# A decoder block of two layers: w_down in two long runs per partition, gate and up columns in a step of seven, and new orders

## The chip, the cores and the metric

The kernel runs on one core of a Trainium2 chip. Its five engines run side by side: TensorE (PE) for matmuls, VectorE (DVE), ScalarE (ACT), GpSimd (POOL), and SyncE (SP), which here only issues DMAs. Each has its own queue of instructions and works through it in order; semaphores tie the queues together. Sixteen DMA engines move data from the main memory into the on-chip memory SBUF (128 partitions). Matmul results land in PSUM. The metric is the device time of one execution in microseconds (us). "Slower" or "faster" is said of a difference over 2%.

## The reference

Four tokens, one per sequence, go through attention, FFN, attention, FFN. Both attentions use the same caches and weights, and so do both FFNs.

```
attention(x): q = x @ wq                      # 16 heads of 256
              k, v = the last 2048 rows of the caches, 8 heads, each used by two heads of q
              o = softmax(q k^T / 16) v
              return o @ wo                   # 4096 -> 448
ffn(x):       return (silu(x @ w_gate) * (x @ w_up)) @ w_down    # 448 -> 1792 -> 448

x = A_x                                       # 4 x 448, bf16
x = x + attention(layernorm(x));  x = x + ffn(layernorm(x))
x = x + attention(layernorm(x));  x = x + ffn(layernorm(x))
```

The window of K and V is 67 MB, more than SBUF holds. Most of it is read for the first attention; what is still in SBUF when the second one comes is used again, and the rest is read a second time.

## The kernel before, in words

The program is a graph of 1465 operations, each with an engine, its inputs and its outputs. The order on each engine is not worked out in the program: it is written out in the lists `SEQ_PE`, `SEQ_DVE`, `SEQ_ACT`, `SEQ_POOL` and `SEQ_SP`, made beforehand by a planner. `schedule` (L240) reads them, puts every K and V load into a slot of SBUF by the list `SLOTS`, makes each load wait for the last reader of what stood in its slot, and places the semaphore waits.

- **Attention.** A pair of heads is a group (`group`, from L957). Each head's K comes in two loads of half a megabyte (L976), each of which DVE transposes in place (L982); V comes in two loads too (L992). PE makes scores (L1016), DVE and PE find the maximum (L1031 to L1045), ACT takes the exponential (L1049), PE turns it (L1060) and multiplies with V (L1090). `out_proj` (L1135, L1143) multiplies with wo and adds into the PSUM bank A.
- **Slots.** There are 31 slots of half a megabyte, and seven more in the space of wq, which come free only after the last query projection of the last token (L683). In each token's first attention, six of eight heads keep their K and V for the second one.
- **FFN of one token** (`ffn`, L783), as soon as its first attention is done. The norm (L589 to L629) feeds the gate and up matmuls (L801). They compute the 1792 hidden values as 14 chunks of 128: for each chunk and each of four pieces of the 448 inputs, 128 columns of w_gate or w_up are loaded into the array as weights, and a small moving operand (32 columns) passes. Gate and up take 112 such pairs together. ACT makes the tanh (L832), DVE the product (L835, L846), and `down_part` (L853) multiplies with w_down, chunk by chunk. Then come the next norm and the query projection (L683 to L722), without which no group of the token's second attention can start.
- The FFNs of tokens 0 to 3 after the first attention are separate; the last FFN takes all four tokens at once and ends the kernel. A second form of the FFN, `ffn_row` (L726), exists in the code, but neither `ROWF` nor `PLAN` names a token for it, so it emits nothing.
- **w_down's layout.** The chunk number of a hidden value is its number divided by 128, its place in the chunk the remainder. SBUF partition p therefore holds rows p, 128 + p, 256 + p and so on, each of 448 values, 896 bytes in a row:

```
            load(rank_d, 1605632, wd_sb[:, :, :], B_w_down.rearrange("(c p) n -> p c n", p=128), "wd", 430)
```

- **Fillers.** A "w" in `SEQ_PE` is a matmul with zero weights into bank A (L1253), put where the planner expected PE to be idle. `HELD` ties operations that read bank A to the fillers.

Of the kernel before, what the change touches and what calls it, by code (L numbers as in the profile page):

```python
# [6 lines left out]
ALU = mybir.AluOpType  # L7
# [6 lines left out]
B = 4  # L14
# [36 lines left out]
ROWF = ()  # L51
# [35 lines left out]
).split()  # L87
SEQ_DVE = (
# [18 lines left out]
).split()  # L107
SEQ_ACT = (
# [5 lines left out]
).split()  # L114
SEQ_POOL = (
# [8 lines left out]
).split()  # L124
SEQ_SP = (
# [243 lines left out]
def build(nc, A_x, A_k_cache, A_v_cache, A_wq, A_wo, B_x, B_w_gate, B_w_up, B_w_down, out):  # L369
# [3 lines left out]
    with ExitStack() as es:  # L373
# [788 lines left out]
        for si, heads in enumerate(rest):  # L1162
# [57 lines left out]
            for t, layer in full:  # L1220
# [7 lines left out]
                if layer == 0:  # L1228
                    if rowf:
# [4 lines left out]
                        for u in with_:  # L1234
                            final(u, pos)
# [94 lines left out]
```

## Time and profile before

| | |
|---|---|
| median of three runs | 278.97 us (278.21 to 281.98) |
| the profiled execution | 279.5 us |
| its span, first to last instruction | 277.7 us |
| mean granted TensorE clock | 0.969 |
| data moved | 96.68 MB, mean 348 GB/s |

The profile is of one execution, so durations are set against 279.5 us, not against the median. In its tables an engine's name with q (SPq) is the engine's sequencer issuing a DMA; PEld is the loading of weights into the array, which runs beside PE's matmuls. A line number stands for the line of the code that made the instruction, and tiles are named "out<-in". In a table by stretch the columns are: the stretch, its length, then for PE, PEld, DVE, ACT and POOL the busy time with the number of instructions, then the granted clock, the busy share of the DMA engines, and GB/s. In a timeline the columns are start, duration, engine, line, operation, tiles, shapes and count; neighbours of one kind are merged into one row, and in brackets stands how long the engine was idle ahead of it and what ended that. The duration of a merged row runs to the end of its last instruction.

### The profile page before, as it was taken

To read this page: it belongs to the slowest core of one execution; us is meant where nothing else is said; L and a number is where in the kernel's file an instruction comes from. 1 tells how busy PE (TensorE), PEld (TensorE's weight loads), DVE (VectorE), ACT (ScalarE), POOL (GpSimd) and SP (SyncE) were. 2 spreads that over 40 slices of the span, in tenths; PEclk is the share of its full clock that TensorE was granted. 3 is DMA by queue.
4 is the path that set the end of the run, shared out by engine and by line. 5 is a ranking of instruction groups with operands and counts; after the bars stand their busy time and mean duration, and the time that the engine had idled before them with its cause. 6 is when DMAs were issued, how large, how long until landed. Compare 5 with 4: busy or idle time off the path is not lost.

```text
span 277.7 us, 9966 instructions
## 1 busy us (share of the span) xinstructions
PE 209.0 (75%) x4424; PEld 125.0 (45%) x4424; DVE 173.8 (63%) x522; ACT 47.3 (17%) x115; POOL 76.5 (28%) x195
## 2 busy tenths in 40 slices
PE   0000076699788968988998897899699798899997
PEld 0000032355464634455754444474454356456694
DVE  7973056445545799368447995655789845559751
ACT  0000000232111220121113221211022031032510
POOL 1000017142204412421253342124132332043650
PEclk9999999999989999999999999999979999599998
DMA  7999999999999999999799999939999999589200
GB/s 292 394 419 412 403 412 406 402 396 401 389 379 405 357 396 415 407 409 353 260 332 410 409 405 411 405 150 362 362 417 407 410 408 346 215 279 408 79 5 1
DMA packets 28474, 96.68 MB, mean 348 GB/s; under 512 B 2828, under 2 KB 6928, under 8 KB 27792
## 3 DMA queue, kind: packets, MB, share of 16 engines
q1 hardware_dynamic: 28423, 96.06, 88.8%
q8 instruction: 34, 0.56, 0.8%
q14 instruction: 9, 0.07, 0.1%
q10 hardware_dynamic: 8, 0.00, 0.0%
HBM read 96.05 MB, written 0.00 MB: 346 GB/s over the span
## 4 chain that ended last, share of the span: by engine, by line
PE 43%; DMA 25%; DVE 13%; SPq 10%; issue 4%; ACT 3%; POOL 2%; ACTq 0%
DMA half<-in_A_k_cache_dram 16%; PE A L1253 10%; DMA half<-in_A_v_cache_dram 9%; PE S L1016 8%; DVE half L982 7%; PE Y L1090 6%; SPq L992 5%; PE Z L801 4%; SPq L976 3%; PE Z L683 3%; SPq L558 2%; PE Z L853 2%; PE A L1143 2%; PE Y L1060 2%; PE A L1135 2%
## 5 line engine op out<-in xcount | busy, mean ns | idle before, releaser
L982 DVE STREAM_TRANSPOSE half<-half 128x1024 uint32<-128x1024 uint32 x80 | 97.2, 1231 | 22.3 <-DMA half<-in_A_k_cache_dram 22.2
L1253 PE MATMUL A<-identb,small 128*128 128x512 bf16 x223 | 67.4, 404 | 0.3 <-DVE xr L903 0.3
L1103 POOL TENSOR_TENSOR small<-small 128x4 f32<-128x4 f32 x32 | 32.5, 1017 | 70.1 <-DVE small L1081 64.7
L1090 PE MATMUL Y<-half,pT 128*8 128x256 bf16 x1024 | 38.7, 275 | 3.2 <-issue 1.4
L1016 PE MATMUL S<-half,qe 128*8 128x256 bf16 (+1 forms) x1120 | 35.3, 269 | 6.3 <-issue 2.0
L1016 PEld LDWEIGHTS S<-half,qe 128*8 128x8 bf16 x1120 | 24.4, 84 | 16.2 <-issue 3.8
L1023 POOL TENSOR_TENSOR qe<-qc,small 128x64 bf16<-128x64 bf16 x56 | 15.3, 295 | 47.6 <-PE S L1016 33.9
L921 PE MATMUL Z<-identb,wo_sb 4*128 4x4 bf16 x4 | 0.3, 167 | 36.7 <-DMA wo_sb<-in_A_x_dram 36.7
L1031 DVE TENSOR_REDUCE small<-S 104x1 bf16<-104x256 f32 x32 | 13.4, 417 | 22.0 <-PE S L1016 22.0
L1090 PEld LDWEIGHTS Y<-half,pT 128*8 128x8 bf16 x1024 | 21.3, 85 | 12.0 <-DVE small L1081 3.2
L1253 PEld LDWEIGHTS A<-identb,small 128*128 128x128 bf16 x223 | 19.1, 103 | 14.9 <-issue 6.4
L1105 ACT ACTIVATE oh<-Y 128x256 bf16<-128x256 f32 x32 | 12.2, 383 | 36.2 <-PE Y L1090 27.2
L615 POOL TENSOR_SCALAR st<-st 128x1 f32<-128x1 f32 x16 | 4.5, 280 | 50.1 <-DVE st L609 50.1
L1107 DVE SCALAR_TENSOR_TENSOR oh<-oh,small,Y 128x256 bf16<-128x256 bf16 x32 | 15.0, 469 | 4.0 <-ACT oh L1105 3.8
L921 PEld LDWEIGHTS Z<-identb,wo_sb 4*128 4x128 bf16 x4 | 0.2, 104 | 36.6 <-DMA wo_sb<-in_A_x_dram 36.6
L1143 PE MATMUL A<-wo_sb,oT 128*4 128x448 bf16 x200 | 13.8, 352 | 1.3 <-DVE oT L1123 1.3
L1049 ACT ACTIVATE praw<-S,small 104x256 bf16<-104x256 f32 x16 | 7.6, 472 | 38.9 <-DVE small L1045 38.9
L1049 ACT ACTIVATE praw<-S,small,st 104x256 bf16<-104x256 f32 x16 | 9.0, 564 | 30.1 <-DVE small L1045 26.6
L1068 ACT ACTIVATE pT<-Y 128x192 bf16<-128x192 f32 x32 | 10.5, 329 | 15.5 <-PE Y L1060 14.1
L683 PE MATMUL Z<-half,small 128*5 128x512 bf16 x160 | 10.9, 379 | 1.5 <-DVE small L592 1.4
L1081 DVE TENSOR_REDUCE small<-Y 128x4 f32<-128x64 f32 x32 | 6.7, 213 | 7.8 <-PE Y L1076 7.6
L1060 PE MATMUL Y<-selt,praw 104*64 104x48 bf16 x256 | 10.1, 197 | 1.8 <-ACT praw L1049 1.7
(135 smaller groups left out, 245.8 us busy)
## 6 DMA issues: line engine op xcount, KB each, us to landing
half<-in_A_v_cache_dram SPq DMA_DIRECT2D x80, 512.0 KB, 13.5
half<-in_A_k_cache_dram SPq DMA_DIRECT2D x76, 512.0 KB, 10.7
wo_sb<-in_A_wo_dram SPq DMA_DIRECT2D x8, 448.0 KB, 11.8
half<-in_A_wq_dram SPq DMA_DIRECT2D x3, 1024.0 KB, 16.2
half<-in_A_k_cache_dram SPq DMA_DIRECT2D x2, 1024.0 KB, 6.4
wd_sb<-in_B_w_down_dram SPq DMA_DIRECT2D x1, 1568.0 KB, 18.5
wu_sb<-in_B_w_up_dram SPq DMA_DIRECT2D x1, 1344.0 KB, 11.8
wg_sb<-in_B_w_gate_dram SPq DMA_DIRECT2D x1, 1344.0 KB, 14.7
```

What stands on the lines that cost most here:

```text
L683: last = e.matmul(zb[32 * j:32 * j + B + 1, 0:512], lhsT=lhsT, rhs=wq_sb[:, c:c + 512], start=(cc == 0), stop=(cc == 3), skip_group_check= ...
L982: return e.transpose(a, a)
L992: g.dma(pp + VLAG, 1 << 19, lambda e, cell=cell, hv=hv, vsrc=vsrc: e.dma_start(unit(cell), vsrc[hv]), None, w=(f"v{t}_{kvh}_{hv}",), run=4 ...
L1016: last = e.matmul(Sb[s_][qd:qd + 8, c0:c0 + rhs.free_size()], lhsT=qe[q_][:, P, ce, :, :].rearrange("p a n -> p (a n)"), rhs=rhs, start=(c ...
L1023: g.op(*((DVE, 0.13) if layer and fresh.get(t, gi) == gi else (POOL, 0.25)), pos - SLEAD - 1, lambda e, P=P, t=t, kvh=kvh: e.tensor_tensor ...
L1049: return e.activation(praw[0:R, 0:128 * n].rearrange("p (g r l) -> p g r l", g=2 * n, l=2), Sb[s_][0:R, 0:128 * n].rearrange("p (l g r) -> ...
L1060: last = e.matmul(Yb[p_][64 * h:64 * h + 64, c0:c0 + (48 if n == 2 else 32)], lhsT=praw[0:R, 64 * gg:64 * gg + 64], rhs=w, start=(gg == 0) ...
L1090: last = e.matmul(Yb[p_][32 * gg:32 * gg + M, 256:512], lhsT=pT[pt][:, gg, 2 * a + hv, 4 * P:4 * P + M] if n == 2 else p1[:, gg % 2, 2 * a ...
L1103: g.op(POOL, 0.69, pos, lambda e: e.tensor_tensor(ri[p_][:, 0:2 * n], rs[p_][:, 0:2 * n], expo[:, 1:1 + 2 * n], op=ALU.pow), r=(f"rs{p_}", ...
L1107: g.op(DVE, 0.43, pos, lambda e: e.scalar_tensor_tensor(out=oh[:, :], in0=oh[:, :], scalar=lomask[:, 0:1], in1=Yb[p_][:, 256:512], op0=ALU ...
L1143: last = e.matmul(Ab[32 * k:32 * k + B, 0:D], lhsT=oT[oi][:, k % 2, k // 2, :], rhs=wo_sb[:, 4 * kvh + k, :], start=False, stop=False, ski ...
L1253: return e.matmul(Ab[:, 0:512], lhsT=zero[:, 0:1].broadcast_to([128, 128]), rhs=identb[:, :].unsqueeze(1).broadcast_to([128, 4, 128]), sta ...
```

## The change

Four things change.

- **The load of w_down.** Hidden value number 896 h + 7 p + j now goes to partition p, chunk 7 h + j. A partition's seven rows of one half then stand side by side in the main memory, and it gets two runs of 6272 bytes instead of 14 of 896.
- **Gate and up.** Chunk 7 h + j now holds the columns 896 h + j + 7 p, so the 128 columns that are loaded as weights are taken in a step of seven instead of one. The numbers of matmuls and weight loads stay, and everything between (tanh, product, the sums of columns kept for the norm) works on chunks as before.
- **`ffn_row`** and what called it are removed.
- **The orders.** All five lists, `SLOTS` and `HELD` are new. The operations are the same; PE has 233 fillers instead of 223, and the last six loads, rather than five, go into the space of wq.

```
-            load(rank_d, 1605632, wd_sb[:, :, :], B_w_down.rearrange("(c p) n -> p c n", p=128), "wd", 430)
+            load(rank_d, 1605632, wd_sb[:, :, :].rearrange("p (h j) n -> p h (j n)", h=2),
+                 B_w_down.rearrange("(h p j) n -> p h (j n)", h=2, j=7), "wd", 6272)
...
                         if cc < 3:
-                            lhsT, x = w[:, cc * FF + fc * 128:cc * FF + fc * 128 + 128], xn[:, cc, sl]
+                            c, x = cc * FF + fc // 7 * 896 + fc % 7, xn[:, cc, sl]
                         else:
-                            lhsT = w[:, 3 * FF + (fc % 7) * 128:3 * FF + (fc % 7) * 128 + 128]
-                            x = xe[:, fc // 7, sl]
+                            c, x = 3 * FF + fc % 7, xe[:, fc // 7, sl]
+                        lhsT = w[:, c:c + 890:7]
                         last = e.matmul((Zb, Z2)[gi][:, k * m * fc:k * m * fc + k * m], lhsT=lhsT,
```

Of the orders, PE's around the FFNs of tokens 1 and 3, by operation number. For token 1, 559 to 568 are gate and up, 655 the scores of a group, 572 to 575 the down projection, 590 to 598 the query; for token 3 they are 1163 to 1172, 1276, 1176 to 1179 and 1194 to 1202.

```
token 1
- 559 560 561 548 627 628 552 562 w w w w w 564 565 566 567 655 563 568 657 w 572 573 574 660 575
+ 559 548 560 561 w 627 628 552 562 564 563 565 566 567 568 w 655 572 573 574 575
token 3
- 1152 1163 1164 1156 1231 1165 1168 1169 1166 1167 1232 1233 1170 1171 1172 w w w w w w 1276 1176 1177 1278 1178 1179
+ 1163 1164 1165 1152 w w w w w 1156 1231 1166 1232 1167 1168 1169 1233 1170 1171 1172 w w w w w w 1176 1177 1178 1179 1276
```

More of the change, by code (lines that the diff above doesn't have):

```diff
@@ L50 @@
 DSTART = 2.1
-ROWF = ()
 COLX = {(3, 1): 2}
@@ L135 @@
     "0 1 2 3 4 5 6 7 8 9 10 11 12 13 14 15 16 17 18 19 20 21 22 23 24 25 26 27 28 29 30 3 4 19 21 22 14 20 9 7 10 21 "
[3 rows of a table removed]
[3 rows of a table added]
 ).split()
 HELD = (
-    "0 44 44 44 94 94 99 99 115 115 119 122 139 139 145 145 195 195 201 201 208 208 213 213 215 215 215 215 215 215 "
-    "215 215"
+    "0 45 45 46 88 89 98 98 116 116 121 126 146 146 152 152 201 201 206 206 220 220 224 224 227 227 227 227 227 227 "
+    "227 227"
 ).split()
@@ L724, in qproj @@
                     ("z2",), tuple(f"qc{t}_{h}" for h in range(HKV)), 0.18, ("Z2",))
-        def ffn_row(ts, rank):
-            rowvec(rvec[:, 1:2], "rvf", ts, rank)
-            g.op(POOL, 0.27, rank, lambda e: e.tensor_single_scalar(rvec[:, 2:3], rvec[:, 1:2], 0.5, op=ALU.mult),
-                 r=("rvf",), w=("rvs",))
-            g.op(POOL, 0.27, rank, lambda e: e.tensor_scalar(rvec[:, 3:4], rvec[:, 1:2], rvec[:, 2:3], None, op0=ALU.mult),
-                 r=("rvf", "rvs"), w=("rvt",))
-            def gu(e, gi, c0, c1):
-                last = None
-                w, zb = (wg_sb, wu_sb)[gi], (Zb, Z2)[gi]
-                for cc in range(c0, c1):
-                    for j in range(4):
-                        f0, f1 = 512 * j, min(512 * j + 512, FF)
-                        if cc < 3:
-                            parts = [(xn[:, cc, 0:B], cc * FF + f0, 0, f1 - f0)]
-                        else:
-                            parts = []
-                            for h in range(2):
-                                a, b = max(f0, 896 * h), min(f1, 896 * h + 896)
-                                if a < b:
-                                    parts.append((xe[:, h, 0:B], 3 * FF + a - 896 * h, a - f0, b - a))
-                        for lhsT, c, o, m in parts:
-                            last = e.matmul(zb[32 * j:32 * j + B, o:o + m], lhsT=lhsT, rhs=w[:, c:c + m],
-                                            start=(cc == 0), stop=(cc == 3), skip_group_check=True)
-                return last
-            for gi, (z, bank, w) in enumerate((("z", "Z", "wg"), ("z2", "Z2", "wu"))):
-                g.op(PE, 1.28, rank, lambda e, gi=gi: gu(e, gi, 0, 3), r=XN[0:B] + (w + "a",), w=(z,), bank=(bank,))
-                g.op(PE, 0.5, rank, lambda e, gi=gi: gu(e, gi, 3, 4), r=XE[0:B] + (w + "b",), acc=(z,), bank=(bank,))
-            g.op(SCA, 0.65, rank, lambda e: e.activation(wide[:, :], Zb[:, :], ACT.Tanh, scale=rvec[:, 2:3]),
-                 r=("z", "rvs"), w=WIDE, bank=("Z",))
-            vec(rank, lambda e: e.scalar_tensor_tensor(out=wide[:, :], in0=wide[:, :], scalar=1.0, in1=Zb[:, :],
-                                                       op0=ALU.add, op1=ALU.mult), ("z",), WIDE, 0.65, ("Z",))
-            vec(rank, lambda e: e.scalar_tensor_tensor(out=wideb[:, 0:512], in0=wide[:, :], scalar=rvec[:, 3:4], in1=Z2[:, :],
-                                                       op0=ALU.mult, op1=ALU.mult), ("z2", "rvt"), WIDE, 0.65, ("Z2",))
-            def turn(e):
-                last = None
-                for c in range(4):
-                    last = e.matmul(Zb[:, 16 * c:16 * c + 16].rearrange("p (j t) -> p j t", j=4),
-                                    lhsT=wideb[:, 128 * c:128 * c + 128], rhs=idt, start=(c == 0), stop=True,
-                                    skip_group_check=True)
-                return last
-            g.op(PE, 0.12, rank, turn, r=WIDE + ("identb",), w=("z",), bank=("Z",))
-            vec(rank, lambda e: e.tensor_copy(hT[:, :], Zb[:, 0:64]), ("z",), ("wb",), 0.13, ("Z",))
-            def down(e):
-                last = None
-                for c in range(4):
-                    for j in range(4):
-                        if 4 * j + c < NFC:
-                            last = e.matmul(Ab[32 * j:32 * j + B, 0:D], lhsT=hT[:, 16 * c + 4 * j:16 * c + 4 * j + 4],
-                                            rhs=wd_sb[:, 4 * j + c, :], start=False, stop=False, skip_group_check=True)
-                return last
-            g.op(PE, 1.5, rank, down, r=("wb", "wd"), acc=tuple(f"row{t}" for t in ts), bank=("A",))
@@ L1163, in build @@
             where = {}
-            if not heads:
-                g.tag = ("f", waiting[-1])
-                ffn_row(waiting, pos)
-                for u in waiting:
-                    rows(u, pos)
-                    residual(u, pos)
-                    final(u, pos)
-                g.tag = None
-                waiting = []
-                continue
             for batch in heads:
@@ L1222, in build @@
                 pos = pos_ - CROSS
-                with_ = []
-                rowf = t in ROWF and layer == 0
                 late = (t, layer) in LATE or layer == 1 and t in fin
                 residual(t, pos, late)
-                norm(t, pos, xr, None if rowf or (layer and not late) else fin.index(t) if layer else -1, late)
+                norm(t, pos, xr, None if layer and not late else fin.index(t) if layer else -1, late)
                 if layer == 0:
-                    if rowf:
-                        ffn_row(with_ + [t], pos)
-                        for u in with_ + [t]:
-                            rows(u, pos)
-                            residual(u, pos, u == t and t in QLATE)
-                        for u in with_:
-                            final(u, pos)
-                    else:
-                        ffn(with_ + [t], pos, late, False)
+                    ffn([t], pos, late, False)
                     norm(t, pos, xr, late=t in QLATE)
```

126 rows, old and new, of tables (SEQ_ACT, SEQ_DVE, SEQ_PE, SEQ_POOL) are left out of this document.

## The prediction

> **What bounds the kernel now.** I read the page first, its totals and its forty slices, to see which resource is full and where it is not.
>
> ```profile
> span 277.7 us, 9966 instructions
> PE 209.0 (75%) x4424; PEld 125.0 (45%) x4424; DVE 173.8 (63%) x522; ACT 47.3 (17%) x115; POOL 76.5 (28%) x195
> PEclk9999999999989999999999999999979999599998
> DMA  7999999999999999999799999939999999589200
> DMA packets 28474, 96.68 MB, mean 348 GB/s; under 512 B 2828, under 2 KB 6928, under 8 KB 27792
> q1 hardware_dynamic: 28423, 96.06, 88.8%
> ```
>
> The DMA engines are full in most slices, with three holes and an empty end. So the time is a stream of 96 MB, plus the time in which the stream starves, plus a tail of computing. The table of busy time by stretch puts numbers on it (GB/s stands last in a row).
>
> ```profile
> 67.00:74.00 7.00, 5.46 (x129) 3.10 (x121) 3.34 (x14) 1.98 (x6) 1.23 (x3) 1.00 1.03 407
> 74.00:81.00 7.00, 6.16 (x155) 4.62 (x155) 4.16 (x14) 0.27 (x1) 1.42 (x4) 0.76 1.07 361
> 81.00:88.00 7.00, 5.96 (x129) 3.73 (x128) 3.23 (x14) 1.40 (x3) 2.35 (x5) 1.00 1.03 407
> 90.00:97.00 7.00, 6.27 (x172) 4.37 (x176) 5.36 (x14) 1.73 (x5) 3.05 (x11) 1.00 0.94 355
> 125.00:147.00 22.00, 20.02 (x494) 13.19 (x486) 12.94 (x44) 3.37 (x9) 7.05 (x20) 1.00 0.89 319
> 180.00:194.00 14.00, 13.18 (x323) 8.94 (x319) 7.96 (x34) 2.06 (x5) 4.35 (x12) 1.00 0.67 261
> 234.00:250.00 16.00, 14.62 (x308) 8.55 (x307) 9.20 (x29) 2.69 (x6) 4.40 (x12) 0.79 0.70 241
> 250.00:259.00 9.00, 8.44 (x207) 5.69 (x211) 8.64 (x27) 2.83 (x7) 4.06 (x13) 1.00 0.92 370
> ```
>
> Undisturbed, the stream runs at 407. Against that, 90 to 97 lacks (407-355)/407 x 7 = 0.9 us, 125 to 147 lacks 4.8, 180 to 194 lacks 5.0 and 234 to 250 lacks 6.5: 17.2 us in all. Each hole lies at the FFN of one token, because slots come free only through attention that waits for the next query. After 259 nothing is left to load, and 19 us of computing follow. The chain that ended last says whose work this is:
>
> ```profile
> PE 43%; DMA 25%; DVE 13%; SPq 10%; issue 4%; ACT 3%; POOL 2%; ACTq 0%
> DMA half<-in_A_k_cache_dram 16%; PE A L1253 10%; DMA half<-in_A_v_cache_dram 9%; PE S L1016 8%; DVE half L982 7%; PE Y L1090 6%; SPq L992 5%; PE Z L801 4%; SPq L976 3%; PE Z L683 3%; SPq L558 2%; PE Z L853 2%; PE A L1143 2%; PE Y L1060 2%; PE A L1135 2%
> ```
>
> L801, the gate and up matmuls, holds 4% of the chain, 11 us. That is where the change touches the computing.
>
> **The load of w_down.** It goes from 1792 rows of 896 bytes to 256 of 6272; the bytes are the same.
>
> ```profile
> L558 SPq DMA_DIRECT2D wd_sb<-in_B_w_down_dram x1: 1398/1398/1398, 63.2 to 63.2; - x1
> DMA to landing us min/median/max: 18.5/18.5/18.5
> ```
>
> ```profile
> 58.58 0.43 SPq L558 DMA_DIRECT2D wo_sb<-in_A_wo_dram  x1
> 63.16 1.40 SPq L558 DMA_DIRECT2D wd_sb<-in_B_w_down_dram  x1
> 64.60 10.86 SPq L976 DMA_DIRECT2D half<-in_A_k_cache_dram  x1
> ```
>
> It is issued at 63.2 and lands at 81.7, so its packets end the slow stretch of 74 to 81. If 6272-byte rows move like the neighbours on both sides, the stretch shrinks by (407-361)/407 x 7 = 0.8 us; if they move no faster, by 0. The packets of 4 KB that fill the neighbours are the nearest row, so I take 0.8. SP's issue should fall from 1.40 to about 0.43, the price of a wo_sb load of 256 rows, but the next instruction on SP then sits 10.86 us, waiting for a slot: worth nothing.
>
> [...]
>
> Who uses the 0.8? PE is in order, so its timeline at token 0 tells:
>
> ```profile
> 77.52 0.91 PE L801 MATMUL Z<-small,wg_sb 128*128 128x32 bf16 x28
> 80.99 0.20 PE L1039 MATMUL S<-identb,small 104*104 104x32 bf16 x1
> 81.71 1.22 PE L853 MATMUL Z<-wide,wd_sb 128*128 128x32 bf16 x42 [0.52 <-DMA wd_sb<-in_B_w_down_dram]
> ```
>
> Token 0's down projection stands 0.52 us for w_down. That wait goes, so token 0's query and the slots it frees (the hole at 90) move up by 0.5, while the stream reaches the hole 0.8 earlier. From 97 on the stream is full to 125, so what it gained passes on. I book -0.7, between 0.5 and 0.8; bounds 0 and -0.8.
>
> **Gate and up columns in a step of seven.** No instruction is added: 112 weight loads and 112 matmuls per FFN, five FFNs. Only the address step of the weight load changes, from 2 to 14 bytes. No load with that step is in the trace, so I bound it. By shape, and on the weight-load timeline:
>
> ```profile
> L801 PEld LDWEIGHTS Z<-small,wg_sb 128*128 128x128 bf16 x280 | 8.3, 99 | 1.0 <-DVE small L875 0.8 <-issue 0.2
> L703 PEld LDWEIGHTS Z<-small,wide 128*128 128x128 bf16 x32 | 1.3, 97 | 2.4 <-ACT wide L694 1.1 <-DVE wide L691 1.0 <-issue 0.2
> L602 PEld LDWEIGHTS Z<-st,small 128*128 128x128 f32 x32 | 5.1, 196 | 3.6 <-DVE st L599 1.7 <-DVE small L592 1.0 <-DVE small L1081 0.4
> ```
>
> ```profile
> 268.16 0.78 PEld L801 LDWEIGHTS Z<-small,wg_sb 128*128 128x128 bf16 x28
> 191.74 0.17 PEld L703 LDWEIGHTS Z<-small,wide 128*128 128x128 bf16 x4 [0.22 <-issue]
> 245.58 0.30 PEld L602 LDWEIGHTS Z<-st,small 128*128 128x128 f32 x2
> ```
>
> From start to start, a contiguous load takes (0.78-0.099)/27 = 25 ns; L703, which takes every second column, (0.17-0.097)/3 = 24 ns: a step of two costs nothing. The dearest full-size load is L602's, in fp32: 0.30-0.196 = 104 ns. So a strided load lies between 25 ns (below that only if a wider step could be quicker than a contiguous one, for which I have no reason) and 104. L703 is the only strided weight load here, so I take 25, cost 0. The upper end is dear, since almost all of it is on the chain: tokens 1, 2, 3 and the last FFN hold 4 x 112 = 448 loads, at 25 ns the 11.2 us that the chain shows. At token 0, gate and up end at 78.43, over 2 us before w_down is there: a cover that hides one slow FFN. At 104 ns the rest pays 448 x 79 ns = 35 us.
>
> **The orders.** SP's first 45 entries are the same and w_down stays 54th; later loads swap places, and slots with them. PE has 233 fillers (L1253) instead of 223. Two changes fall into holes of the stream, and are priced from PE's timeline:
>
> ```profile
> 131.39 1.24 PE L1253 MATMUL A<-identb,small 128*128 128x512 bf16 x5
> 132.46 1.55 PE L801 MATMUL Z<-small,wu_sb 128*128 128x32 bf16 x56
> ```
>
> ```profile
> 238.66 2.72 PE L1253 MATMUL A<-identb,small 128*128 128x512 bf16 x6
> 241.31 1.51 PE L1016 MATMUL S<-half,qe 128*8 128x256 bf16 x32
> 242.76 0.87 PE L853 MATMUL Z<-wide,wd_sb 128*128 128x32 bf16 x28
> ```
>
> With them go SP's issue of the loads that those scores free, the last transpose of the chain, and the stretch's granted clock (ahead of DMA share and GB/s):
>
> ```profile
> 243.25 1.39 SPq L976 DMA_DIRECT2D half<-in_A_k_cache_dram  x3
> ```
>
> ```profile
> 256.98 1.15 DVE half L982
> ```
>
> ```profile
> 235.40:242.30 6.90, 6.13 (x96) 3.02 (x96) 4.01 (x6) 0.27 (x1) 0.70 (x2) 0.51 0.68 235
> ```
>
> Token 1: the five fillers between gate and up go (132.46-131.39 = 1.1 us), one comes ahead; its chain gains 0 to 0.9. I take -0.5, since the activation behind it must still be awaited. Token 3: five fillers are added ahead (1.1), and the scores of the group behind go from ahead of the down projection to behind it. Down and query come 1.5 - 1.1 = 0.4 earlier; but those scores free slots, so four loads come 1.1 + 1.4 = 2.5 later (1.4 is the 56 down matmuls), and on SP all others queue behind them. Six loads rather than five go into the space of wq, free only after the last query; the last K tile is the eighth of the final ten rather than the seventh, one load of 0.52 MB at 407 GB/s, 1.3 us. So it lands up to 3.8 us later. What hides this is DVE, busy 8.64 of 9 us from 250 to 259; in the chain the last transpose starts at 256.98, 2.7 us after the seventh load can land (243.25 + 2 + 7 x 1.3 = 254.3, with 2 us to landing as my estimate). Loss 0 to 1.1; I take +0.3.
>
> On the clock I take 0: it fell to 0.51 under token 3, so that six fillers took 2.72 us instead of 6 x 0.215 = 1.3. Five full-width fillers ahead may hold it up (-2) or only cost (already counted). The other swaps, those of DVE, ACT and POOL among them, I put at 0, within -3 and +3, a sixth of the starved 17.2 either way: no row prices them. The removed row form issued nothing.
>
> Sum: -0.7 + 0 - 0.5 + 0.3 = -0.9. The profiled execution took 279.5 us (span 277.7 and 1.8 around it), 0.5 above the median of 278.97; on the median this gives **278.1 us**. A measurement here tells about 2% (5.6 us) from no change: 273.4 and 284.5 are the bounds.
>
> **Rivals.**
> *The strided weight load is dear (slower).* Place: L801 of tokens 1 to 3 and of the end. For it: the 448 loads have nothing to hide behind, and 14 bytes is far from any step in the trace. Against it: a step of 4 bytes costs nothing. It becomes "slower" when a load takes 6.4 us / 448 = 14 ns more, so at 39 ns. At twice the time, 50 ns, it adds 448 x 25 ns = 11.2: 289 us; at 104 ns, 313. Chance 0.21.
> [...]
>
> *Nothing is gained.* The rows land earlier but the stream then starves 0.8 longer at 90, and the order is neutral: 279.0. For it: all four holes are set by token chains. Against it: w_down is itself awaited at 81.2. Chance 0.2.
>
> *The new order starves the stream more*: late scores of token 3, last K tile, other swaps, at 1.1 + 3 from their bounds: 282. Chance 0.14.
>
> *The new order fills the holes and holds the clock*: -0.8 - 0.9 - 2 - 3 = -6.7, 272. For it: 17.2 us are there to be won. Against it: the chains that make the holes keep all their instructions. Chance 0.08.
>
> **How the numbers follow.** The forecast has 0.37, in 275.5 to 280. "Nothing" and "starves more" stay within 2%; 0.37 + 0.2 + 0.14 = 0.71. Faster 0.08, slower 0.21. From 274 to 288 leaves out most of the faster case (0.06) and the dear loads from nearly twice the time on (0.14).
>
> **What would show it.** Packets should fall to 28474-1792+256 = 26938. GB/s while w_down flows should be above 400, its wait at L853 gone. L801's weight loads should keep 0.78 us per 28; 1.4 us or more means the rival. The holes should stay near 17 us, and the span behind the last landing near 19. I am wrong if L801 has more than 5% of the chain, or if the holes move by over 3 us.

## The result, and the profile after

The changed kernel takes **300.17 us** (median of six runs, 298.23 to 302.67) against 278.56 for the kernel before (six runs, 277.49 to 281.98). The ratio is **1.079, with an interval of 1.073 to 1.085**: 22 us slower, and above the forecast range. Ratios, here and below, leave disturbed runs out, so they can differ a little from the quotient of two medians.

From the page after, the totals, the granted clock, the DMA rows and the packets:

```profile
span 298.4 us, 10118 instructions
PE 233.0 (78%) x4498; PEld 143.9 (48%) x4498; DVE 175.2 (59%) x522; ACT 47.1 (16%) x115; POOL 76.4 (26%) x195
PEclk9999999999569997995799999999999987799966
DMA  7999999999979999983699999549999995397000
DMA packets 26938, 96.70 MB, mean 324 GB/s; under 512 B 2827, under 2 KB 5135, under 8 KB 26255
DMA half<-in_A_k_cache_dram 22%; PE A L1178 11%; PE Z L746 10%; PE S L961 7%; PE Y L1035 6%; DVE half L927 6%; SPq L937 5%; SPq L921 3%; PE A L1088 2%; PE Z L798 2%; PE Z L683 2%; SPq L557 2%; PE A L1080 2%; PE Y L1005 2%; DVE small L976 1%
```

The packets fell to 26938, so w_down does come in long rows. The holes in the DMA row are deeper. On the chain, the gate and up matmuls (L801 before, L746 now) went from 4% to 10%, which the prediction named as the sign of the dear weight load. The view by shape and the weight-load timeline of the FFN of token 2 confirm it:

```profile
L746 PEld LDWEIGHTS Z<-small,wg_sb 128*128 128x128 bf16 x280 | 16.3, 154 | 1.3 <-DVE small L820 1.1 <-issue 0.2
L746 PEld LDWEIGHTS Z<-small,wu_sb 128*128 128x128 bf16 x280 | 15.7, 153 | 0.6 <-issue 0.4
```

```profile
189.00 1.57 PEld L746 LDWEIGHTS Z<-small,wg_sb 128*128 128x128 bf16 x28
190.64 1.64 PEld L746 LDWEIGHTS Z<-small,wg_sb 128*128 128x128 bf16 x28
192.65 3.23 PEld L746 LDWEIGHTS Z<-small,wu_sb 128*128 128x128 bf16 x56
```

From start to start a load now takes (1.57-0.154)/27 = 52 ns by the first row, and 55 and 56 by the others; in the kernel before, the rows gave 25 to 29. The pace was about the same at two granted clocks: here the clock was 1.00, as the third row of the next table shows, and under token 0 (the first row), where PE's timeline gives 53 ns, it was 0.50. The table of busy time by stretch shows where the time is lost (clock, DMA share and GB/s stand last):

```profile
74.00:81.00 7.00, 6.68 (x101) 5.72 (x101) 3.24 (x10) 0.00 (x0) 1.42 (x4) 0.50 1.02 409
81.00:99.00 18.00, 16.98 (x339) 10.13 (x338) 10.43 (x34) 3.44 (x8) 4.67 (x14) 0.82 0.86 326
188.00:196.00 8.00, 7.74 (x152) 7.30 (x152) 4.06 (x12) 0.00 (x0) 1.61 (x6) 1.00 0.34 134
126.00:154.00 28.00, 27.57 (x531) 17.95 (x529) 13.34 (x47) 4.07 (x10) 7.34 (x17) 0.82 0.69 251
186.00:206.00 20.00, 18.89 (x364) 13.70 (x364) 10.67 (x40) 2.06 (x5) 4.41 (x12) 1.00 0.60 219
242.00:265.00 23.00, 22.57 (x400) 14.93 (x401) 10.62 (x38) 2.33 (x6) 5.06 (x15) 0.78 0.64 226
265.00:276.00 11.00, 8.85 (x226) 5.92 (x219) 8.39 (x25) 3.48 (x9) 3.56 (x9) 1.00 0.84 325
276.00:282.00 6.00, 5.53 (x152) 3.46 (x140) 4.23 (x23) 2.64 (x6) 3.49 (x6) 1.00 0.02 5
```

Set against a full 409 GB/s, the holes are 3.7 us (81 to 99), 10.8 (126 to 154), 9.3 (186 to 206) and 10.3 + 2.3 (242 to 276), 36 us in all. In the same way, with the stretch from 250 to 259 added, before had 18. The tail behind the last landing grew from 18.7 to 22.4 us. That makes 18 + 4 = 22, a little more than the 20.7 by which the span grew; 74 to 81, where w_down flows, now runs at 409 instead of 361, so 0.8 came back.

### The profile page after: what moved, and what is told of

Read it like the earlier page. It is cut to its first block, busy times and chain, and to the rows that moved or that the text cites. A ratio compares the mean times of both kernels' runs of the same rounds, so it can differ in the third digit from the quotient of the medians.

```text
span 298.4 us, 10118 instructions
## 1 busy us (share of the span) xinstructions
PE 233.0 (78%) x4498; PEld 143.9 (48%) x4498; DVE 175.2 (59%) x522; ACT 47.1 (16%) x115; POOL 76.4 (26%) x195
## 2 busy tenths in 40 slices
DMA packets 26938, 96.70 MB, mean 324 GB/s; under 512 B 2827, under 2 KB 5135, under 8 KB 26255
## 4 chain that ended last, share of the span: by engine, by line
PE 50%; DMA 22%; DVE 10%; SPq 10%; issue 2%; ACT 2%; POOL 2%; DVEq 0%; ACTq 0%
DMA half<-in_A_k_cache_dram 22%; PE A L1178 11%; PE Z L746 10%; PE S L961 7%; PE Y L1035 6%; DVE half L927 6%; SPq L937 5%; SPq L921 3%; PE A L1088 2%; PE Z L798 2%; PE Z L683 2%; SPq L557 2%; PE A L1080 2%; PE Y L1005 2%; DVE small L976 1%
## 5 line engine op out<-in xcount | busy, mean ns | idle before, releaser
L1178 PE MATMUL A<-identb,small 128*128 128x512 bf16 x233 | 73.9, 419 | 2.1 <-issue 1.7
L961 PE MATMUL S<-half,qe 128*8 128x256 bf16 (+1 forms) x1184 | 37.4, 274 | 6.1 <-DVE half L927 4.8
L961 PEld LDWEIGHTS S<-half,qe 128*8 128x8 bf16 x1184 | 26.3, 88 | 16.0 <-DVE half L927 7.5
L1178 PEld LDWEIGHTS A<-identb,small 128*128 128x128 bf16 x233 | 20.3, 107 | 18.1 <-issue 9.9
L746 PE MATMUL Z<-small,wg_sb 128*128 128x32 bf16 x280 | 16.7, 209 | 0.5 <-DVE small L820 0.5
L746 PEld LDWEIGHTS Z<-small,wg_sb 128*128 128x128 bf16 x280 | 16.3, 154 | 1.3 <-DVE small L820 1.1
L746 PE MATMUL Z<-small,wu_sb 128*128 128x32 bf16 x280 | 16.1, 210 | 0.0
L746 PEld LDWEIGHTS Z<-small,wu_sb 128*128 128x128 bf16 x280 | 15.7, 153 | 0.6 <-issue 0.4
```

The costliest lines, as they stand in the source:

```text
L746: last = e.matmul((Zb, Z2)[gi][:, k * m * fc:k * m * fc + k * m], lhsT=lhsT, rhs=x.unsqueeze(2).broadcast_to([128, k, m]), start=(fc == 0 ...
L961: last = e.matmul(Sb[s_][qd:qd + 8, c0:c0 + rhs.free_size()], lhsT=qe[q_][:, P, ce, :, :].rearrange("p a n -> p (a n)"), rhs=rhs, start=(c ...
L1178: return e.matmul(Ab[:, 0:512], lhsT=zero[:, 0:1].broadcast_to([128, 128]), rhs=identb[:, :].unsqueeze(1).broadcast_to([128, 4, 128]), sta ...
```

## The experiments

Where a run leaves its FFN with shuffled or doubled hidden values, its expectation says so; the instructions and transfers are those named. Ratios are to the kernel before, run on the same chip.

### Taking the change apart: step, rows, orders

The first run keeps the change and undoes the orders:

```
-SEQ_PE, SEQ_DVE, SEQ_ACT, SEQ_POOL, SEQ_SP, SLOTS, HELD of the changed kernel
+the same seven lists of before
```

> The changed kernel (w_down in 6272-byte runs, columns in a step of seven) with all orders, slots and filler ties of before. Theory A, the strided weight load with all that follows from it is the whole loss: 298 to 301 us, as with the new orders. Rival B, the loads alone cost 448 x 28 ns = 12.6 us and the new orders the other 9: about 291 us.

The second has the lists alone:

```
-SEQ_PE, SEQ_DVE, SEQ_ACT, SEQ_POOL, SEQ_SP, SLOTS, HELD of before
+the same seven lists of the changed kernel
```

> The kernel before (896-byte runs, contiguous columns) with the new orders alone. Theory A: 277 to 280 us, no change that can be told. Rival B: 285 to 288 us.

The third and the fourth keep the long runs and take the step away, with the old and with the new lists:

```
-                            c, x = cc * FF + fc // 7 * 896 + fc % 7, xn[:, cc, sl]
+                            c, x = cc * FF + fc * 128, xn[:, cc, sl]
...
-                            c, x = 3 * FF + fc % 7, xe[:, fc // 7, sl]
-                        lhsT = w[:, c:c + 890:7]
+                            c, x = 3 * FF + fc % 7 * 128, xe[:, fc // 7, sl]
+                        lhsT = w[:, c:c + 128]
```

> Orders of before, w_down in 6272-byte runs, but gate and up columns contiguous, so the hidden values meet the wrong rows of w_down and the output is that of a shuffled FFN; every instruction and transfer is there. Both theories: 0 to 0.8 us below before (277.8 to 278.6), with the wait of the first down projection gone. A third possibility, that the long rows themselves hurt: above 280.

> The changed kernel with its new orders and its long runs, only the columns contiguous (shuffled FFN, as in the run with the old orders). Theory A: 276 to 279 us, all of the loss gone with the step. Rival B: 284 to 288 us.

| | step | rows of w_down | orders | median us | ratio, interval |
|---|---|---|---|---|---|
| changed kernel | 7 | 6272 B | new | 300.17 | 1.079 (1.073 to 1.085) |
| step and rows | 7 | 6272 B | before | 298.18 | 1.073 (1.065 to 1.082) |
| orders alone | 1 | 896 B | new | 280.27 | 1.007 (1.002 to 1.012) |
| rows alone | 1 | 6272 B | before | 278.64 | 1.001 (0.997 to 1.005) |
| rows and orders | 1 | 6272 B | new | 279.48 | 1.004 (1.000 to 1.009) |

Theory A holds and rival B falls: with either set of orders the loss appears with the step of seven and goes with it. The orders cost 0.7% on their own (0.5 to 3.2 us), the wrong way for the -0.2 that was forecast; the two runs with the new orders and a step of one end 0.3 and 0.5 us above the ranges that Theory A gave them. The long rows do nothing that can be told, within -0.8 and +1.3 us. They do what they should where they flow. Here are the stretches of the run with the long rows alone, and w_down's view of what PE waited for:

```profile
74.00:81.00 7.00, 5.65 (x161) 4.72 (x161) 4.06 (x13) 0.34 (x2) 1.65 (x6) 0.76 1.03 411
81.00:88.00 7.00, 6.53 (x148) 4.58 (x152) 3.77 (x18) 1.24 (x3) 1.57 (x3) 1.00 1.00 393
55.00:62.00 7.00, 6.66 (x139) 4.01 (x141) 1.83 (x7) 1.50 (x4) 2.54 (x9) 0.88 0.90 319
```

```profile
L798 PEld LDWEIGHTS Z<-wide,wd_sb x280: 95/96/118, 82.9 to 274.0; 128*128 128x128 bf16 x140
  DVE wide L774: 0.6, 1
  DVE wide L791: 0.3, 2
  issue: 0.2, 1
```

The rate is 411 instead of 361, and w_down no longer stands among the waits. But in this execution the stream had lost (411-319)/411 x 7 = 1.6 us at 55 to 62, before w_down flowed, at a lowered clock (0.88). Single executions differ by more than this term is worth.

What the wait was worth at token 0 itself can be read from a run of a later section, with the long rows, the step of seven at tokens 1 to 3 alone, and the orders of before. Its last gate matmuls of token 0 start at 77.56, those of before at 77.52, but its down projection starts thus:

```profile
80.89 1.22 PE L798 MATMUL Z<-wide,wd_sb 128*128 128x32 bf16 x42
```

That is 0.8 us ahead of the 81.71 of before, and the last transposition of the query (L717) keeps the lead, at 88.12 against 88.94. The scores in front end 0.2 earlier; the other 0.6 is about the 0.52 that the prediction saw as the wait. So the gain came at token 0, in this one trace; that it reaches the end of the kernel is not shown.

### Which steps are dear

In the kernel before, the gate and up columns are read with another step for each token (L799 is here what L801 was):

```
-                            lhsT, x = w[:, cc * FF + fc * 128:cc * FF + fc * 128 + 128], xn[:, cc, sl]
...
+                        s = (2, 3, 4, 5, 6)[4 if last else ts[0]]
+                        c = (0, 1536, 3328, 4224)[cc] + fc % 7
+                        lhsT = w[:, c:c + 127 * s + 1:s]
```

> The kernel before, with the gate and up columns read in a step of 2, 3, 4, 5 and 6 for tokens 0, 1, 2, 3 and the last FFN (other columns than the reference's, as many loads). Theory A1, a load is slow once fewer than two columns share 16 bytes: 25 ns for steps 2, 3 and 4, more for 5 and 6, where it rises with the number of 16-byte lines touched. Rival A2, slow as soon as the step is odd or not a power of two: 25 ns for 2 and 4, about 53 for 3, 5 and 6. Rival A3, a smooth rise with the step: 25, 30, 36, 42, 47.

> The same with steps of 8, 10, 12, 14 and 16 columns for tokens 0 to 3 and the last FFN. A1: 53 to 56 ns for all of them, since each column stands in a line of its own as nearly all do at seven. A3: 60 to over 100 ns, rising.

The runs took 283.49 and 303.93 us, one execution each, beside 277.29 for before. From the weight-load timeline of the first, one row for each of the steps 2 to 6, and from that of the second, for 8 to 16:

```profile
76.89 1.20 PEld L799 LDWEIGHTS Z<-small,wu_sb 128*128 128x128 bf16 x42
133.62 1.62 PEld L799 LDWEIGHTS Z<-small,wu_sb 128*128 128x128 bf16 x56 [0.24 <-DVE st L609]
184.97 2.13 PEld L799 LDWEIGHTS Z<-small,wu_sb 128*128 128x128 bf16 x56
236.58 1.21 PEld L799 LDWEIGHTS Z<-small,wu_sb 128*128 128x128 bf16 x28
274.02 1.42 PEld L799 LDWEIGHTS Z<-small,wu_sb 128*128 128x128 bf16 x28
```

```profile
77.54 2.63 PEld L799 LDWEIGHTS Z<-small,wu_sb 128*128 128x128 bf16 x42
140.71 3.31 PEld L799 LDWEIGHTS Z<-small,wu_sb 128*128 128x128 bf16 x55 [0.27 <-issue]
196.70 3.32 PEld L799 LDWEIGHTS Z<-small,wu_sb 128*128 128x128 bf16 x55 [0.26 <-issue]
252.69 1.78 PEld L799 LDWEIGHTS Z<-small,wu_sb 128*128 128x128 bf16 x28
293.57 1.82 PEld L799 LDWEIGHTS Z<-small,wu_sb 128*128 128x128 bf16 x28
```

Less one load's own length (0.12 us on the mean in the first run, 0.164 in the second) and divided by the other loads, the rows give a pace; steps 1 and 7 are from the traces of before and of the changed kernel. Most other rows of these traces lie within 6 ns of it. With contiguous columns, the rows in the places of steps 2 and 3 took 1.20 and 1.67 us. The third line is worked out: 128 columns of two bytes in a step of s touch 16 s pieces of 16 bytes, and 128 at most.

| step, columns | 1 | 2 | 3 | 4 | 5 | 6 | 7 | 8 | 10 | 12 | 14 | 16 |
|---|---|---|---|---|---|---|---|---|---|---|---|---|
| ns a load | 25 to 29 | 26 | 27 | 37 | 40 | 48 | 52 to 56 | 60 | 58 | 58 | 60 | 61 |
| pieces touched | 16 | 32 | 48 | 64 | 80 | 96 | 112 | 128 | 128 | 128 | 128 | 128 |

In these runs the pace followed the pieces of 16 bytes, about half a nanosecond each (37 ns for 64, 60 for 128), but did not go under 25 ns, and it stood still from eight columns on (58 to 61), where each has a piece of its own. Steps up to three stayed at this floor (26 and 27). A2 falls (3 is cheap, 4 is not). A3 had steps 2 to 6 within 3 ns, and falls by the second run, which shows no rise beyond 8. A1 is right in kind and wrong at step 4, which it had at 25 ns (two columns in each piece are not enough), and a little low from 8 on. That it is the pieces, and not something else that grows with the step, is a fit to these numbers and no more.

### Where the step costs, by token

The step stays in some FFNs and goes from the others; orders of before and long runs throughout:

```
-                        lhsT = w[:, c:c + 890:7]
+                        s = 7 if not last and ts[0] == 0 else 1       # the other two runs: ts[0] > 0; last
...
+                        lhsT = w[:, c:c + 127 * s + 1:s]
```

> Orders of before, long runs, the step of seven for token 0's FFN alone, contiguous columns elsewhere (there the hidden values meet the wrong rows of w_down). Theory C, the prediction's cover: token 0's slow loads (112 x 28 ns = 3.1 us) hide behind the wait for w_down, 278 to 279.5 us. Rival D, no cover: the scores that stand behind them in PE's order free slots, so their delay opens a hole in the DMA stream at 81 to 88 us: 282 to 284 us.

> As before this one, but the step of seven for tokens 1 to 3 alone. By the loads alone 3 x 3.1 = 9.4 us: 288 us. If the lowered clock under the slow loads costs on top: 290 to 293.

> The step of seven for the last FFN alone, orders of before, long runs. By the loads alone 3.1 us: 281.8. With a lowered clock for the fillers and the down projection behind: 282.5 to 283.5.

The us lost are the ratio less one, times the 278.4 of before (278.7 in the last row).

| step of seven in | median us | ratio, interval | us lost | loads x 28 ns |
|---|---|---|---|---|
| token 0 | 281.46 | 1.011 (1.006 to 1.015) | 3.0 | 3.1 |
| tokens 1 to 3 | 290.93 | 1.045 (1.040 to 1.050) | 12.5 | 9.4 |
| the last FFN | 282.75 | 1.018 (1.013 to 1.024) | 5.1 | 3.1 |
| all five | 298.18 | 1.073 (1.065 to 1.082) | 20.5 | 15.7 |

The parts add up: 3.0 + 12.5 + 5.1 = 20.6. Token 0 is not covered, so C falls and D holds, if a little cheaper than it said. PE's timeline of that run, and its stretches, say why:

```profile
79.59 1.65 PE L746 MATMUL Z<-small,wg_sb 128*128 128x32 bf16 x28
81.18 1.88 PE L961 MATMUL S<-half,qe 128*8 128x256 bf16 x32
```

```profile
74.00:81.00 7.00, 6.84 (x117) 6.24 (x116) 3.16 (x9) 0.00 (x0) 1.42 (x4) 0.56 1.02 410
81.00:88.00 7.00, 6.77 (x131) 4.19 (x129) 3.40 (x16) 1.08 (x3) 1.02 (x1) 0.71 0.80 290
```

In PE's timeline of before, the scores that are L961 here are L1016:

```profile
79.33 1.04 PE L1016 MATMUL S<-half,qe 128*8 128x256 bf16 x29 [0.68 <-issue]
```

Behind token 0's gate and up stand these scores of a group of token 1 (before, three of the 32 ran just ahead of this row). Before, they ended at 79.33 + 1.04 = 80.4; now they end at 83.1, and the slots that they free come 2.7 us later. In 81 to 88 the stream falls to 290 GB/s, where the same stretch before had 407: (407-290)/407 x 7 = 2.0 of the 3.0 us. The prediction looked at what waits for w_down, and not at what else stands behind the slow loads in PE's queue.

Tokens 1 to 3 and the last FFN lose more than their loads; both medians lie where their expectations put a lowered clock on top. Under the last FFN part of it can be seen: here is PE's timeline of the run with the step there.

```profile
267.24 1.65 PE L746 MATMUL Z<-small,wg_sb 128*128 128x32 bf16 x28
...
276.54 1.01 PE L1178 MATMUL A<-identb,small 128*128 128x512 bf16 x2
277.48 0.28 PE L852 MATMUL Z<-identb,xs 128*16 128x128 bf16 x1
```

And here is that of before:

```profile
268.18 0.85 PE L801 MATMUL Z<-small,wg_sb 128*128 128x32 bf16 x28
...
274.21 0.59 PE L1253 MATMUL A<-identb,small 128*128 128x512 bf16 x2
274.74 0.22 PE L907 MATMUL Z<-identb,xs 128*16 128x128 bf16 x1
```

From its first gate matmul to the last transposition the FFN takes 277.48 - 267.24 = 10.2 us there, and 274.74 - 268.18 = 6.6 in the profile of before. The loads explain 3.1 of 3.7, and two fillers, slowed from 0.59 to 1.01 us, another 0.4. The rest of the 5.1 these two executions do not show.

The run with the step at tokens 1 to 3 can be read in the same way, from an FFN's first gate matmul to the last transposition of its query (L717). Here are token 1's rows in that run, with the five fillers between gate and up:

```profile
128.34 2.42 PE L746 MATMUL Z<-small,wg_sb 128*128 128x32 bf16 x42 [0.26 <-DVE small L820]
132.83 2.29 PE L1178 MATMUL A<-identb,small 128*128 128x512 bf16 x5
148.54 0.23 PE L717 MATMUL Z<-wide,fold 128*32 128x128 bf16 x4
```

And here are those of before (its fillers, 1.24 us, stand in the prediction):

```profile
129.03 1.22 PE L801 MATMUL Z<-small,wg_sb 128*128 128x32 bf16 x42 [0.26 <-DVE small L875]
142.82 0.23 PE L717 MATMUL Z<-wide,fold 128*32 128x128 bf16 x4
```

Token 1 takes 20.2 us instead of 13.8, token 2 17.0 instead of 12.5, and token 3 18.3 instead of 16.1. That is 6.4 + 4.5 + 2.2 = 13.1 us, which accounts for the 12.5 lost. The loads are 3.1 of each. Token 1's other 3.3 came at a granted clock of 0.50 on the mean of 128.3 to 141, where before had 1.00 (129 to 135.9): the fillers took 2.29 us instead of 1.24, and the scores behind 1.88 instead of 1.08. At token 3 the clock was low in both runs (0.51 from 235.4 to 242.3 in before), with six fillers at 2.72 us in each, and before lost 0.77 us there to a stall of PE that the profile does not explain.

### Is it the time on PE, or the clock?

With the step of seven the granted clock fell from 0.97 to 0.92 on the mean; what lowers it, no run here shows. To hold the time on PE nearly equal with twice the matmuls, contiguous loads and matmuls are done twice:

```
-                for cc in range(c0, c1):
-                    for fc in range(NFC):
+                for cc, fc in [(cc, fc) for cc in range(c0, c1) for _ in range(2) for fc in range(NFC)]:
...
```

> The kernel before with every gate and up weight load and matmul done twice (the hidden values come out doubled): two contiguous loads, 50 to 53 ns, for each of 53 ns in a step of seven, but the array works twice as often. Theory E, only the time on PE counts: 296 to 299 us, as with the step of seven and the same orders. Rival F, part of the loss is the clock that drops when the array waits for weights: 290 to 294 us, with a granted clock near that of before (0.97) instead of 0.92.

It took 296.51 us, ratio 1.065 (1.060 to 1.070), 18.0 us more, at a mean granted clock of 0.954. All five FFNs hold 560 loads: that is 18.0 for 560 x 25 ns = 14.0 us of added PE time, 1.3 us lost per us; with the step of seven and the same orders it was 20.5 for 560 x 28 = 15.7, again 1.3. By the time, Theory E is the closer, and F's 290 to 294 was missed. But the run isn't clean. In PE's timeline of it,

```profile
82.25 0.75 PE L1017 MATMUL S<-half,qe 128*8 128x256 bf16 x19
85.56 0.60 PE L1017 MATMUL S<-half,qe 128*8 128x256 bf16 x13 [2.56 <-issue]
```

PE stood 2.56 us for nothing that the profile shows, in the middle of the scores that free slots. Without that, the run could be up to 2.6 us faster, at the upper edge of F's range (if the executions that were not profiled stalled too), so the time does not settle it. Token 1, which this stall does not touch, says more. These are its fillers in this run:

```profile
139.09 1.24 PE L1254 MATMUL A<-identb,small 128*128 128x512 bf16 x5
```

They take 1.24 us, as in the kernel before. With doubled loads the FFN of token 1 takes 17.1 us, 3.3 more than before, at a granted clock of 0.83 from 134.7 to 145; with the step of seven it took 6.4 more, at 0.50. So by its size F is right for token 1: about half of its loss there is the time of instructions at a lowered clock. In the run with the step of seven everywhere and the orders of before, token 1 takes 4.7 us more, so this share differs between executions. How much of the whole 20.5 it is, and what lowers the clock, stays open; that both runs lose 1.3 us per us of loads may be partly chance, since one of them has the stall.

### A version at the free steps

The table of steps suggests a layout whose runs are longer than before and whose steps are free. Orders are those of before:

```
-                 B_w_down.rearrange("(h p j) n -> p h (j n)", h=2, j=7), "wd", 6272)
+            blocks = ((0, 3), (3, 2), (5, 2))          # first chunk and chunks of a block; one transfer each
...
+                        off, s = (((0, 3),) * 3 + ((3, 2),) * 2 + ((5, 2),) * 2)[fc % 7]
+                        c = 128 * off + fc % 7 - off
...
+                        lhsT = w[:, c:c + 127 * s + 1:s]
```

> A full kernel, orders of before: the seven chunks of a half are split into blocks of 3, 2 and 2, so w_down comes in runs of 2688 and 1792 bytes (three transfers) and gate and up columns in steps of 3 and 2, which cost 26 to 28 ns a load where each token has one step. If only the number of 16-byte lines under a load counts: within 1 us of before, 277.5 to 279.5. If any step other than 1 or 2 were dear, or three transfers were: above 282.

It took 278.90 us (12 runs), against 279.54 for before (17); the ratio is 1.005 (0.999 to 1.012). Its stretch where w_down flows:

```profile
74.00:81.00 7.00, 6.55 (x157) 4.71 (x156) 4.13 (x15) 0.27 (x1) 1.42 (x4) 0.76 1.04 394
```

The stream gets 394 GB/s instead of 361, and the loss is gone, so the steps of 3 and 2 are cheap in a whole kernel too. No gain on before can be told, and a loss of up to 1.2% is not excluded.

## Why the prediction was wrong

- **What bounds the kernel** stood. Time is a full stream plus holes plus a tail; 18 us of the loss are holes, 4 are tail.
- **The load of w_down**: the rate (409 against 361) and the vanished wait came as written, and so did the packets. From 74 to 81 all five traces with 896-byte rows show 360 to 365 GB/s, and all seven with 6272-byte rows 409 to 412. The -0.7 isn't contradicted, and isn't shown: measured -0.8 to +1.3.
- **The weight load in a step of seven: this step failed.** The text bounded it between 25 and 104 ns and took 25, because the one strided load of the trace, with a step of two, cost that. It is 52 to 56, about 28 ns more. For the 448 loads counted, that is 12.5 us instead of 0. A step of two says nothing about a step of seven, since both may lie on different sides of an edge, and in the table of steps the pace begins to rise between three (27 ns) and four (37).
- **The cover at token 0** failed too: priced at 0, it cost 3.0 us, since scores behind the slow loads free slots.
- **The clock**, taken at 0, failed as well: at token 1 it fell to 0.50 under the slow loads, and about 3 us of that token's loss went with it in the run with the step at tokens 1 to 3. That fillers hold it up, the -2 of one rival, is not shown: in the profile after, it was 0.66 from 243 to 257.6, around the gate and up of token 3.
- **The rival** "strided weight load is dear" was the right one, with the right place and nearly the right size per load, and too low in the sum: 289 us for twice the time, where 300 was measured. It left out token 0 and counted each load once, with no lowered clock behind; the runs by token give 560 loads x 28 ns x 1.3 = 20.4, and the rest of the 22 is about what the orders cost alone. Its chance of 0.21 was too small for a term whose ends lay 35 us apart with one row at the near end.
- **The orders**: -0.2 forecast, +0.5 to +3.2 measured alone. Small, and of the wrong sign; which of the swaps does it was not tried. By its number, "starves more" was the better rival there. The 2 us to landing in the reckoning of token 3 is what the shortest V load of before shows: 3.3 us from issue to landing, less 1.3 for its 0.52 MB at 407 GB/s.

## What to carry to other kernels

A layout that makes a transfer contiguous can make the reader of the tile strided, and the reader may run five times where the transfer runs once: price the reader first, with the row that has the very step, or by a short run with one step per FFN. When work on an in-order engine grows, look at everything that stands behind it in the queue, and above all at what frees buffers; here a us of added weight loading cost 1.3 on the whole, a lowered clock included. Where a term has no row and its upper end is large, the chance should lean on the width of the bounds and not on the nearest row.

## What was not expected of the hardware

The pace of 128-column bf16 weight loads, each with its small matmul, followed the number of 16-byte pieces touched, for steps of 1 to 16 columns: a floor of 25 to 29 ns up to step 3, 37 at 4, 52 to 56 at 7, about 60 from 8 on, flat to 16. The pace of the step of seven was about the same at full and at half granted clock: 52 to 56 ns under token 2, at 1.00, and under token 0, at 0.50, by this row of PE's timeline of the changed kernel, (2.40-0.21)/41 = 53 with 0.21 for one matmul:

```profile
78.20 2.40 PE L746 MATMUL Z<-small,wu_sb 128*128 128x32 bf16 x42
```
